# Threshold attention with a gated MLP: weights kept in their parts' storage, low words scaled on VectorE, a stacked 64-token unit, and a new planned order

## The chip, the core and the metric

The kernel runs on one core of one Trainium2 chip. The metric is the device time of one execution in microseconds (us); the time of a kernel is the median over several executions. A core has TensorE (PE in the profile; PEld are its weight loads), VectorE (DVE), ScalarE (ACT), GpSimd (POOL), and SyncE (SP), which here only issues DMA transfers.

## What is computed

The reference, cut to what matters (8 batches, 8 heads, 576 tokens, head width 64, so x is 8 x 576 x 512):

```python
scores = 0.125 * q @ k.T                                   # per head
thresh = max(scores, axis=-1) - tau
scores = where(scores >= thresh, scores, -1e9)
attn = softmax(scores);  x = attn @ v                      # heads side by side
h = gelu_tanh(x @ w_in);  u, v = h[:, :512], h[:, 512:]    # w_in: 512 x 1024
v = (v - mean(v)) / sqrt(var(v) + 1e-6) * g_ln
v = w_sg @ v + b_sg                                        # over the 576 tokens
out = x + (u * v) @ w_out                                  # w_out: 512 x 512
```

w_in and w_out arrive as 64-bit floats, and the kernel gets them as pairs of 32-bit words.

## The kernel before, in words

**Attention.** Step `attention(n)` handles two heads at once (n runs from 0 to 31, four of them make a batch). Each n has nine tiles of 128 queries by 576 keys. For a tile PE computes the scores, DVE takes the row maximum (`nm`), ACT the exponentials (`p`), POOL the threshold (written beside `nm`), and DVE multiplies by the comparison and sums (`SCALAR_TENSOR_TENSOR p`). PE then transposes `p` with an identity, ACT copies the transposed blocks out of PSUM (`pt`, `tt`), and PE multiplies by the values (`rv`) in two parts of 256 and 320 queries. The values' product has 64 output rows per head; the two heads stand in the two halves of the PE array. DVE multiplies the result by the inverse sums (`x32`), and x is split into a high part `xh` (ACT) and a rest `xl` (POOL) in the fast 32-bit format of PE.

Queries and keys are split in the same way (`qhi`, `khi` on ACT, the rest on POOL) and laid out by DMA into `qst`, `ks` and `klz`. The first n is computed without the split, straight from the loaded `rq` and `rk`.

**MLP.** `moe(b)` follows when the four attention steps of its batch are through. Units `v0` to `v3` multiply 128 tokens by the second half of w_in, `v4` the last 64 tokens; then come gelu, the normalisation and the split into `z` (`zt` for the 64 tokens). Units `u` multiply by the first half of w_in, `y` mix the tokens with `w_sg`, `o` multiply by w_out and add x. Every product of two split matrices is three matmuls: high by high, rest by high, high by rest. A unit of w_in has four blocks of 128 input columns and so 12 matmuls; `v4` has 12 too, with 64 output rows.

**Weights.** `from_double` makes the high part and the rest of one 128 x 512 block from its two words per number, 12 blocks in all: ACT takes the magnitude of the upper word (L551) and scales the low word (L552); DVE assembles the 32-bit number in four instructions (L557, L559, L561, L563); POOL multiplies the scaled low word by the number's power of two (L569) and adds it (L570); ACT copies the high part (L571) and POOL subtracts it (L572). The raw words of all 18 weight loads wait in four buffers that the `z` tiles use later.

**Order.** All steps are recorded with a nominal time. A planner (`Planner`) plays the program through with costs of its own and picks, for each engine, the next step among those that are ready, by nominal time plus an offset for the kind of step (table `OFF`, table `START` for the MLP's units). The engines execute their instructions in the order that comes out. DMA transfers are all issued by SP, in order.

Of the kernel before, what the change touches and what calls it, by code (L numbers as in the profile page):

```python
# [12 lines left out]
F32 = mybir.dt.float32  # L13
F32R = mybir.dt.float32r
# [6 lines left out]
P = 128  # L21
# [32 lines left out]
}  # L54
LAST_SCALE, SIGMA, SPREAD = 0.55, 1.155, 0.7
LOOK = dict(tensor=117.6, vector=64.6, scalar=38.8, gpsimd=48.8, sync=843.3)
# [23 lines left out]
WINDOW, WINDOW_BUSY, CLOCK, STREAM = 10240 / 3, 3200 * P, 2.4, 2.185  # L80

# [83 lines left out]
class Planner:  # L165
# [51 lines left out]
    def _record(self, engine, op, out, args, accum_out, kw):  # L217
# [26 lines left out]
        for t, entry in done:  # L244
# [5 lines left out]
                         P if engine == "tensor" else first.shape[0], engine == "vector" and ports > 1))  # L250
# [26 lines left out]
    def order(self):  # L277
# [14 lines left out]
        turn = dict(vector=0.0, gpsimd=0.0)  # L292
# [28 lines left out]
        def run(i):  # L321
# [8 lines left out]
            for k in self.steps[i]:  # L330
# [75 lines left out]
def tile_threshold_attention_gated_mlp(  # L406
# [89 lines left out]
    wih = [cpool.tile([P, DF], F32R, name=f"wih{c}") for c in range(NC)]  # L496
    wil = [cpool.tile([P, DF], F32R, name=f"wil{c}") for c in range(NC)]
    woh = [cpool.tile([P, DM], F32R, name=f"woh{c}") for c in range(NF)]
    wol = [cpool.tile([P, DM], F32R, name=f"wol{c}") for c in range(NF)]
# [31 lines left out]
    def raw_weights(k, w):  # L531
        return cpool.tile([P, 2 * FH], F32, tag=f"z{k % NM}", name=f"w{k}")[:, 0:w]

    spare = ([(mtmp, "mt0", FH), (mtmp, "mt1", FH), (mtmp, "gt0", FH)],
             [(mpool, "gh0", S), (mpool, "gl0", S), (mtmp, "gt1", FH)],
             [(mpool, "gh1", S), (mpool, "gl1", S), (xpool, "xl6", S)])

    def from_double(src, hi, lo, j, put, time, k):

        t = {}  # L540

        def load():
            t["raw"] = raw_weights(k, 2 * FH).bitcast(U32)
# [4 lines left out]
        def magnitude():  # L548
            t["full"], t["rest"], t["pow"] = (
                pool.tile([P, w], F32, tag=tag, name=f"w{k}{tag}")[:, 0:FH] for pool, tag, w in spare[j])  # L550
            nc.scalar.activation(t["full"], t["up"].bitcast(F32), AF.Abs, scale=UPPER_MORE)  # L551
            nc.scalar.activation(t["rest"], t["low"], AF.Copy, scale=2.0 ** -52)  # L552
# [16 lines left out]
        put("w_mul", time, lambda: nc.gpsimd.tensor_tensor(t["rest"], t["rest"], t["pow"], ALU.mult))  # L569
        put("w_add", time, lambda: nc.gpsimd.tensor_tensor(t["full"], t["full"], t["rest"], ALU.add))  # L570
        put("w_hi", time, lambda: nc.scalar.activation(hi, t["full"], AF.Copy))  # L571
# [683 lines left out]
```

## Time and profile before

| what | value |
|---|---|
| median of 3 runs | 1037.2 us (1036.03 to 1037.33) |
| the profiled execution | 1032.46 us, of which the span of the program's instructions is 1030.4 us |
| clock granted to TensorE, mean of the span | 0.99 |

The profiled execution is 4.7 us faster than the median of the timed runs. The profile's engine rows count a matmul as busy until its modelled end, so that consecutive matmuls overlap in the rows; the distance from start to start is what one of them costs when PE is full. "Idle before" stands for the time that an engine waited ahead of an instruction, and the arrow names what ended the wait.

### The profile page before, as it was taken

Reading aid. Unit: us, or ns where it says so; the run is one execution under the profiler, and the core shown is the slowest. Engines: PE = TensorE matmul, PEld = TensorE weight load, DVE = VectorE, ACT = ScalarE, POOL = GpSimd, SP = SyncE. Lnnn points to the kernel's source line nnn. Section 1 sums busy time; section 2 is a strip of 40 time slices with the busy share of each in tenths; the row PEclk is TensorE's granted clock in tenths of the full one; section 3 lists DMA queues with packets and bytes.
Section 4 is the critical chain, followed back from the end, with each engine's and each line's share of the span. In section 5 each row is a group of like instructions: output and inputs, shape, how many; then the busy total and the mean of one; then the engine's idle time right before and its main releaser. Section 6 shows DMA issues by size and latency. Waiting matters only on the chain.

```text
span 1030.4 us, 20086 instructions
## 1 busy us (share of the span) xinstructions
PE 973.8 (95%) x6972; PEld 836.2 (81%) x6972; DVE 654.6 (64%) x1399; ACT 695.5 (67%) x1489; POOL 617.1 (60%) x1089
## 2 busy tenths in 40 slices
PE   3768799999999999999999999999999999999997
PEld 2556578898788987889778897889878897789887
DVE  5777787755777637765576656776377655774350
ACT  4768778764877658766687648776587766865452
POOL 5878667555663666555675556645665556634566
PEclk9889999999999999999999999999999999999999
DMA  8464433444135423344144431344323441310001
GB/s 263 138 185 125 116 86 103 103 108 107 43 83 128 119 72 81 88 128 109 31 103 110 108 97 45 89 116 121 84 74 90 124 118 31 91 34 24 18 6 46
DMA packets 50758, 96.42 MB, mean 94 GB/s; under 512 B 8033, under 2 KB 16225, under 8 KB 50658
## 3 DMA queue, kind: packets, MB, share of 16 engines
q1 hardware_dynamic: 50658, 95.15, 35.0%
q8 instruction: 55, 0.90, 0.4%
q14 instruction: 45, 0.37, 0.1%
HBM read 38.44 MB, written 9.44 MB: 46 GB/s over the span
## 4 chain that ended last, share of the span: by engine, by line
PE 75%; DVE 6%; ACT 6%; POOL 6%; DMA 3%; issue 3%; SPq 1%; POOLq 0%; DVEq 0%; ACTq 0%
PE all_banks L992 37%; PE all_banks L908 13%; PE all_banks L758 13%; PE all_banks L522 12%; DVE p L800 2%; ACT pt L878 2%; POOL vv L1071 2%; ACT p L793 1%; DVE nm L767 1%; DMA qst<-qhi 1%; DMA ks<-khi 1%; POOL ot L1172 1%; DMA g_bc<-in_g_ln 1%; DVE x L920 1%; ACT vv L1068 1%
## 5 line engine op out<-in xcount | busy, mean ns | idle before, releaser
L800 DVE SCALAR_TENSOR_TENSOR p<-all_banks,nm,p 128x576 f32<-128x576 f32 x256 | 207.0, 814 | 87.7 <-ACT p L793 36.1
L767 DVE TENSOR_REDUCE nm<-all_banks 128x1 f32<-128x576 f32 x288 | 212.8, 750 | 47.7 <-PE all_banks L758 38.8
L793 ACT ACTIVATE p<-all_banks,nm 128x576 f32<-128x576 f32 x256 | 188.5, 746 | 28.4 <-DVE nm L767 27.8
L758 PE MATMUL all_banks<-ks,qst 128*128 128x288 f32 x620 | 190.3, 325 | 13.4 <-DVE p L800 5.4
L522 PE MATMUL all_banks<-ident_r,p 128*128 128x128 f32 x1152 | 173.5, 282 | 21.9 <-DVE p L800 20.5
L878 ACT ACTIVATE pt<-all_banks 128x512 f32<-128x512 f32 (+1 forms) x320 | 168.4, 557 | 29.4 <-PE all_banks L522 28.2
L758 PE MATMUL all_banks<-klz,qst 128*128 128x288 f32 x620 | 173.5, 297 | 0.0
L522 PEld LDWEIGHTS all_banks<-ident_r,p 128*128 128x128 f32 x1152 | 139.9, 145 | 38.6 <-DVE p L800 20.7
L758 PEld LDWEIGHTS all_banks<-ks,qst 128*128 128x128 f32 x620 | 118.3, 191 | 38.4 <-ACT pt L878 11.3
L908 PE MATMUL all_banks<-pt,rv 128*64 128x320 f32 (+1 forms) x1024 | 138.3, 412 | 1.1 <-ACT pt L878 1.1
L758 PEld LDWEIGHTS all_banks<-klz,qst 128*128 128x128 f32 x620 | 118.7, 191 | 0.4
L773 POOL TENSOR_TENSOR nm<-columns,nm 128x1 f32<-128x1 f32 x288 | 55.7, 197 | 100.0 <-DVE nm L767 89.8
L992 PE MATMUL all_banks<-wsh,z 128*128 128x288 f32 (+2 forms) x512 | 112.8, 296 | 0.3 <-POOL z L1084 0.3
L908 PEld LDWEIGHTS all_banks<-pt,rv 128*64 128x64 f32 x1024 | 67.8, 136 | 50.3 <-issue 8.7
L992 PEld LDWEIGHTS all_banks<-wsh,z 128*128 128x128 f32 x512 | 85.4, 188 | 0.7 <-POOL z L1084 0.5
L992 PE MATMUL all_banks<-xh,wih 128*128 128x288 f32 (+2 forms) x256 | 78.4, 306 | 3.8 <-ACT pt L878 3.8
L1144 POOL TENSOR_TENSOR gl<-uu,gh 128x288 fp32r<-128x288 f32 (+2 forms) x64 | 51.5, 807 | 49.7 <-ACT gh L1140 46.4
L978 DVE SCALAR_TENSOR_TENSOR gt<-gt,all_banks 128x512 f32<-128x512 f32 (+1 forms) x40 | 27.2, 681 | 78.4 <-ACT gt L971 78.4
L992 PE MATMUL all_banks<-xl,wih 128*128 128x288 f32 (+2 forms) x256 | 76.4, 299 | 0.0
L992 PE MATMUL all_banks<-gh,woh 128*128 128x288 f32 (+2 forms) x256 | 76.2, 298 | 0.0
L992 PE MATMUL all_banks<-xh,wil 128*128 128x288 f32 (+2 forms) x256 | 75.9, 297 | 0.0
L992 PE MATMUL all_banks<-gl,woh 128*128 128x288 f32 (+2 forms) x256 | 75.4, 295 | 0.0
(222 smaller groups left out, 2223.8 us busy)
## 6 DMA issues: line engine op xcount, KB each, us to landing
rk<-in_kT SPq DMA_DIRECT2D x32, 320.0 KB, 2.9
rv<-in_vP SPq DMA_DIRECT2D x32, 320.0 KB, 2.9
ks<-khi SPq DMA_DIRECT2D x62, 160.0 KB, 2.8
rq<-in_qT SPq DMA_DIRECT2D x32, 288.0 KB, 3.3
qst<-qhi SPq DMA_DIRECT2D x62, 144.0 KB, 2.4
qst<-rq SPq DMA_DIRECT2D x62, 144.0 KB, 2.4
ks<-khi SPq DMA_DIRECT2D x62, 144.0 KB, 2.9
out_T<-ot SPq DMA_DIRECT2D x56, 144.0 KB, 1.8
```

The lines of the kernel that those rows point to most:

```text
L522: nc.tensor.transpose(out, x, ident_r.bitcast(F32))
L758: nc.tensor.matmul(sc[:, a, 0:HALF], w, x, start=(j == 0), stop=(j == len(terms) - 1))
L767: nc.vector.tensor_reduce(nmax, st["s", h, i][:, :, 0:HALF], AX.XY, ALU.max, negate=True)
L773: nc.gpsimd.tensor_tensor(thr, toff, st["nm", h, i], ALU.subtract)
L793: nc.scalar.activation(target(h, i), st["s", h, i][:, :, 0:HALF], AF.Exp, bias=st["nm", h, i])
L800: nc.vector.scalar_tensor_tensor(dst, st["s", h, i][:, :, 0:HALF], st["thr", h, i], dst, ALU.is_ge, ALU.mult, accum_out=st["l", p][:, c:c ...
L878: nc.scalar.activation(dst, src, AF.Copy)
L908: nc.tensor.matmul(acc[h * D:(h + 1) * D, 0:w], st["v"][:, o:o + D], unit(h, p)[:, kt, 0:w] if kt < NM else tail_unit(p)[:, 0:w], start=(k ...
L978: put("stt1", end, lambda: nc.vector.scalar_tensor_tensor(t["tmp"], t["tmp"], GELU_C, t["acc"], ALU.add, ALU.mult))
L992: nc.tensor.matmul(st["acc"], *term(j), start=(j == 0), stop=(j == n - 1))
L1071: nc.gpsimd.tensor_tensor(st["v", i], st["v", i], g_bc[0:rows], ALU.mult)
L1144: nc.gpsimd.tensor_tensor(st["gl", p, d], st["u", p, d], st["gh", p, d], ALU.subtract)
```

## The change

1. The raw words of a block are loaded into the storage that its high part and rest will have (`raw_wi01` becomes `wi01`), so that the twelve loads need no shared buffers. The scratch of the conversion moves to other tiles (`wz`, `wt`).
2. The scaling of the low word on ACT and the multiply on POOL become one `scalar_tensor_tensor` on DVE (L589 of the new file), which reads the low word and the power of two.
3. xh and xl of a head pair become one tile `x` of 640 columns; the rests of the last 64 tokens are written a second time (`xt`, POOL, L956), beside their high parts. `v4` then multiplies 128 stacked rows (64 high, 64 rests) by the high weights, and 64 rows by the rests of the weights: 8 matmuls in place of 12. ACT copies the lower 64 rows of the result (`mlow`, L1001) and DVE adds them to the upper ones (`madd`, L1004) ahead of the gelu.
4. The planner adds 92 ns when PE goes to the half-array matmuls and 220 ns when it comes back; `OFF`, `START` and `LOOK` hold new numbers.
5. A few scratch tiles have other homes (the query tails, the last outputs).

```diff
-LOOK = dict(tensor=117.6, vector=64.6, scalar=38.8, gpsimd=48.8, sync=843.3)
+LOOK = dict(tensor=20.8, vector=91.4, scalar=115.7, gpsimd=100.2, sync=4015.6)
+DRAIN = (92.0, 220.0)
...
+                    if ops[k][6] != self.tiled:
+                        start += DRAIN[not ops[k][6]]
+                        self.tiled = ops[k][6]
...
-            t["raw"] = raw_weights(k, 2 * FH).bitcast(U32)
+            t["raw"] = cpool.tile([P, 2 * FH], F32, tag=home, name=f"raw_{home}").bitcast(U32)
...
-            nc.scalar.activation(t["rest"], t["low"], AF.Copy, scale=2.0 ** -52)
...
-        put("w_mul", time, lambda: nc.gpsimd.tensor_tensor(t["rest"], t["rest"], t["pow"], ALU.mult))
-        put("w_add", time, lambda: nc.gpsimd.tensor_tensor(t["full"], t["full"], t["rest"], ALU.add))
-        put("w_hi", time, lambda: nc.scalar.activation(hi, t["full"], AF.Copy))
-        put("w_lo", time, lambda: nc.gpsimd.tensor_tensor(lo, t["full"], hi, ALU.subtract))
+        put("w_mul", time, lambda: nc.vector.scalar_tensor_tensor(
+            t["pow"], t["low"], 2.0 ** -52, t["pow"], ALU.mult, ALU.mult))
+        put("w_add", time, lambda: nc.gpsimd.tensor_tensor(t["full"], t["full"], t["pow"], ALU.add))
+
+        def hi_part():
+            parts_of[home] = cpool.tile([P, 2 * FH], F32R, tag=home, name=home)
+            nc.scalar.activation(parts_of[home][:, 0:FH], t["full"], AF.Copy)
...
+                        x = x_of[b, hp] = xpool.tile([P, S + KW], F32R, tag=f"x{n % 7}", name=f"x{n}")
+                        xh_of[b, hp], xl_of[b, hp] = x[:, 0:S], x[:, KW:S + KW]
...
+                    nc.gpsimd.tensor_tensor(x_of[b, hp][:, S:KW], st["x", p][:, w - TAIL:w], xh_of[b, hp][:, MAIN:S],
+                                            ALU.subtract)
...
+        def lower_half():
+            t["h"] = tile_of()
+            nc.scalar.activation(t["h"], acc_of()[TAIL:P], AF.Copy)
+
+        def add_halves():
+            nc.vector.tensor_tensor(t["h"], acc_of()[0:TAIL], t["h"], ALU.add)
...
+            def tail_term(j):
+                c, k = divmod(j, 2)
+                if k == c // (NC - 1):
+                    return x_of[b, c][:, MAIN:KW], w_in_of(0, c, slice(FH, DF))
+                return xh_of[b, c][:, ts_], w_in_of(1, c, slice(FH, DF)), TAIL
...
+                acc = products(put, time, spread, f"v{b}_{i}", (P, FH), tail_term, 2 * NC)
```

What moves, first on DVE at the start of the program, where n = 0 is under way (`nm0_0_1` is the row maximum of head 0, tile 1; `w0`, `w1`, `w2` before and `wt1`, `wt2`, `wt3` now are weight blocks in conversion). Before:

```order
L800 SCALAR_TENSOR_TENSOR p0_0_195,l0_0_196<-all_banks_91,nm0_1_0_193,p0_0_195 128x576
L561 SCALAR_TENSOR_TENSOR w0mt0_198<-w0_164,w0mt0_198 128x512
L557 TENSOR_SCALAR w1gh0_214<-w1gh0_214 128x512
L563 TENSOR_SCALAR w0gt0_200<-w0mt0_198 128x512
L559 TENSOR_SCALAR w1gh0_214<-w1gh0_214 128x512
L557 TENSOR_SCALAR w2gh1_221<-w2gh1_221 128x512
L561 SCALAR_TENSOR_TENSOR w1gh0_214<-w1_166,w1gh0_214 128x512
L559 TENSOR_SCALAR w2gh1_221<-w2gh1_221 128x512
L563 TENSOR_SCALAR w1gt1_216<-w1gh0_214 128x512
L561 SCALAR_TENSOR_TENSOR w2gh1_221<-w2_168,w2gh1_221 128x512
L767 TENSOR_REDUCE nm0_0_1_265<-all_banks_91 128x1
```

Now, the same place:

```order
L827 SCALAR_TENSOR_TENSOR p0_0_177,l0_0_178<-all_banks_91,nm0_1_0_175,p0_0_177 128x576
L794 TENSOR_REDUCE nm0_0_1_194<-all_banks_91 128x1
L577 TENSOR_SCALAR wt1h_191<-wt1h_191 128x512
L794 TENSOR_REDUCE nm0_1_1_211<-all_banks_91 128x1
L579 TENSOR_SCALAR wt1h_191<-wt1h_191 128x512
L827 SCALAR_TENSOR_TENSOR p0_1_205,l0_0_178<-all_banks_91,nm0_0_1_194,p0_1_205 128x576
L581 SCALAR_TENSOR_TENSOR wt1h_191<-raw_wi00_153,wt1h_191 128x512
L827 SCALAR_TENSOR_TENSOR p0_1_205,l0_0_178<-all_banks_91,nm0_1_1_211,p0_1_205 128x576
L583 TENSOR_SCALAR wt1l_192<-wt1h_191 128x512
L577 TENSOR_SCALAR wt2_231<-wt2_231 128x512
L577 TENSOR_SCALAR wt3h_244<-wt3h_244 128x512
```

Nine weight instructions stood ahead of the second tile's first maximum; now none does, and the weights come between and behind. Up to the first instruction of the first MLP batch's gelu DVE executes 48 weight instructions before (all of them) and 55 now: 11 blocks with five each, the twelfth block later.

Second on SP, at the start (`rv` are values, `w0` to `w3` and `raw_wi00`, `raw_wi10` are weight loads of 512 KB each, `qst` the first laid-out queries). Before:

```order
L576 DMA g_bc_103<-in_g_ln 128x512
L546 DMA w0_164<-in_w_in 128x1024
L546 DMA w1_166<-in_w_in 128x1024
L546 DMA w2_168<-in_w_in 128x1024
L546 DMA w3_171<-in_w_in 128x1024
L658 DMA rv0_177<-in_vP 128x640
L658 DMA rv1_183<-in_vP 128x640
L697 DMA qst01_131<-qhi1_186 64x576
L697 DMA qst11_133<-qhi1_186 64x576
```

Now:

```order
L603 DMA g_bc_103<-in_g_ln 128x512
L685 DMA rv0_148<-in_vP 128x640
L685 DMA rv1_150<-in_vP 128x640
L564 DMA raw_wi00_153<-in_w_in 128x1024
L564 DMA raw_wi10_156<-in_w_in 128x1024
L724 DMA qst01_115<-qhi1_162 64x576
L724 DMA qst11_117<-qhi1_162 64x576
```

Two weight loads stand ahead of the laid-out queries where there were four.

Third on PE, the 64-token unit of the second batch. Before:

```order
L992 MATMUL all_banks_91<-wih0_104,xh4_1500 64x512
L992 MATMUL all_banks_91<-wil0_108,xh4_1500 64x512
L992 MATMUL all_banks_91<-wih0_104,xl4_1511 64x512
L992 MATMUL all_banks_91<-wih1_105,xh5_1792 64x512
L992 MATMUL all_banks_91<-wil1_109,xh5_1792 64x512
L992 MATMUL all_banks_91<-wih1_105,xl5_1816 64x512
L992 MATMUL all_banks_91<-wih2_106,xh6_2098 64x512
L992 MATMUL all_banks_91<-wil2_110,xh6_2098 64x512
L992 MATMUL all_banks_91<-wih2_106,xl6_2143 64x512
L992 MATMUL all_banks_91<-wih3_107,xh7_2866 64x512
L992 MATMUL all_banks_91<-wil3_111,xh7_2866 64x512
L992 MATMUL all_banks_91<-wih3_107,xl7_2868 64x512
```

Now (`wi01` holds the high part and the rest of one block):

```order
L1035 MATMUL all_banks_91<-wi01_950,x4_1378 128x512
L1035 MATMUL all_banks_91<-wi01_950,x4_1378 64x512
L1035 MATMUL all_banks_91<-wi11_1076,x5_1711 128x512
L1035 MATMUL all_banks_91<-wi11_1076,x5_1711 64x512
L1035 MATMUL all_banks_91<-wi21_1221,x6_2213 128x512
L1035 MATMUL all_banks_91<-wi21_1221,x6_2213 64x512
L1035 MATMUL all_banks_91<-wi31_1267,x7_2827 64x512
L1035 MATMUL all_banks_91<-wi31_1267,x7_2827 128x512
```

Four matmuls are gone, and full and half widths alternate.

More of the change, by code (lines that the diff above doesn't have):

```diff
@@ L249, in _record @@
         self.ops.append((self.current, engine, time_of(engine, op, first, reads), needs,
-                         P if engine == "tensor" else first.shape[0], engine == "vector" and ports > 1))
+                         P if engine == "tensor" else first.shape[0], engine == "vector" and ports > 1,
+                         engine == "tensor" and op != "transpose" and args[0].dtype == F32
+                         and min(first.shape[0], args[0].shape[0]) < P))
     def rehearse(self, plan):
@@ L495, in tile_threshold_attention_gated_mlp, with w_in_of, w_out_of @@
     g_bc = cpool.tile([P, FH], F32, name="g_bc")
[L496 to L499, printed above, removed]
+    parts_of = {}
+    def w_in_of(k, c, cs):
+        half = cs.start // FH
+        return parts_of[f"wi{c}{half}"][:, k * FH + cs.start - half * FH:k * FH + cs.stop - half * FH]
+    def w_out_of(k, c, ms):
+        return parts_of[f"wo{c}"][:, k * DM + ms.start:k * DM + ms.stop]
     wsh = [cpool.tile([P, S], F32R, name=f"wsh{c}") for c in range(NM)]
@@ L529, in threshold_offset, with spare, spares, from_double @@
         at("tau", 0.0, lambda: nc.vector.tensor_tensor(toff, toff, tau_sb, ALU.subtract))
[L531 to L540, printed above, removed]
+    used = [0]
+    def spare():
+        used[0] += 1
+        return used[0]
+    def spares(k, w):
+        if k % 3 == 2:
+            both = xpool.tile([P, S + KW], F32, tag="x6", name=f"wt{k}")
+            return both[:, 0:w], both[:, S:S + w]
+        return [mpool.tile([P, S], F32, tag=f"g{x}{k % 3}", name=f"wt{k}{x}")[:, 0:w] for x in "hl"]
+    def from_double(src, home, early, put, time, k):
+        t, sp = {}, None if early else spare()
         def load():
-            t["raw"] = raw_weights(k, 2 * FH).bitcast(U32)
+            t["raw"] = cpool.tile([P, 2 * FH], F32, tag=home, name=f"raw_{home}").bitcast(U32)
             words = t["raw"].rearrange("p (c w) -> p c w", w=2)
@@ L548, in magnitude @@
         def magnitude():
-            t["full"], t["rest"], t["pow"] = (
-                pool.tile([P, w], F32, tag=tag, name=f"w{k}{tag}")[:, 0:FH] for pool, tag, w in spare[j])
+            if early:
+                both = cpool.tile([P, 2 * FH], F32, tag=f"z{k % NM}", name=f"wz{k}")
+                t["full"], t["pow"] = both[:, 0:FH], both[:, FH:2 * FH]
+            else:
+                t["full"], t["pow"] = spares(sp, FH)
             nc.scalar.activation(t["full"], t["up"].bitcast(F32), AF.Abs, scale=UPPER_MORE)
-            nc.scalar.activation(t["rest"], t["low"], AF.Copy, scale=2.0 ** -52)
         def word(step):
@@ L580, in weights @@
                 cs = slice(o, o + FH)
-                jobs.append(partial(from_double, w_in[c * P:(c + 1) * P, cs], wih[c][:, cs], wil[c][:, cs], len(jobs) % 3))
+                jobs.append(partial(from_double, w_in[c * P:(c + 1) * P, cs], f"wi{c}{o // FH}", o == FH))
         for c in range(NM):
@@ L602, in tail_weights @@
     def tail_weights(put, time, k):
-        t = {}
+        t, sp = {}, spare()
         def load():
-            t["raw"] = raw_weights(k, S)
+            t["raw"] = spares(sp, S)[0]
             for d0 in (0, TAIL):
@@ L973, in gate @@
         def gate():
-            t["h"] = tile_of()
+            if not halves:
+                t["h"] = tile_of()
             nc.vector.scalar_tensor_tensor(t["h"], t["tmp"], 1.0, t["acc"], ALU.add, ALU.mult)
+        if halves:
+            put("mlow", end, lower_half)
+            put("madd", end, add_halves)
         put("msq", end, square)
@@ L991, in f @@
                 for j in range(lo, hi):
-                    nc.tensor.matmul(st["acc"], *term(j), start=(j == 0), stop=(j == n - 1))
+                    w, x, *rows = term(j)
+                    nc.tensor.matmul(st["acc"][0:rows[0]] if rows else st["acc"], w, x, start=(j == 0), stop=(j == n - 1))
             return f
@@ L1023, in w_part @@
         def w_part(cs):
-            return lambda k, c: (wih, wil)[k][c][:, cs]
+            return lambda k, c: w_in_of(k, c, cs)
         def v_unit(put, time, i):
@@ L1043, in new @@
                 return st["v", i]
-            gelu2(put, end, acc, new, f"{b}_{i}")
+            gelu2(put, end, acc, new, f"{b}_{i}", i == NM)
             def stats():
@@ L1164, in evacuate @@
                 if last and p:
-                    tag = ("x32", "y32", "ir")[m % 3]
-                    st["o", p, m] = xtmp.tile([P, S - 2 * P], F32, tag=tag, name=f"ot{b}_{p}_{m}")
+                    st["o", p, m] = xpool.tile([P, S + KW], F32, tag=f"x{4 + m % 3}", name=f"ot{b}_{p}_{m}")[:, 0:spans[p][1]]
                 else:
```

65 lines of the change are left out of this document (36 added, 29 removed), and 20 rows, old and new, of the table START.

## The prediction

> **What bounds the kernel now.** I read the busy time by stage first. The columns are the stretch, its length, then busy time and instructions of PE, PE's weight loads, DVE, ACT and POOL, the granted clock, the DMA share and GB/s:
>
> ```profile
> 0.00:20.00 20.00, 9.37 (x33) 6.13 (x33) 10.35 (x24) 8.65 (x14) 9.84 (x25) 1.00 0.87 261
> 20.00:60.00 40.00, 21.41 (x124) 15.90 (x125) 29.63 (x54) 27.05 (x53) 34.84 (x42) 0.87 0.59 168
> 60.00:134.00 74.00, 59.47 (x407) 46.86 (x408) 57.48 (x121) 56.47 (x118) 53.17 (x83) 0.93 0.47 126
> 134.00:200.00 66.00, 64.95 (x458) 52.09 (x457) 51.69 (x114) 54.41 (x118) 42.24 (x81) 1.00 0.44 109
> 200.00:980.00 780.00, 775.32 (x5667) 675.02 (x5667) 491.19 (x1060) 528.91 (x1148) 444.79 (x819) 1.00 0.33 85
> 980.00:1031.00 51.00, 43.30 (x290) 40.24 (x288) 14.29 (x30) 19.98 (x41) 32.24 (x42) 0.99 0.08 27
> ```
>
> From 134 us on PE is full: 5.7 us idle in the 846 us up to 980. There a matmul less is time saved, and DVE (63%), ACT and POOL have room. In the first 134 us PE is idle for 43.8 us (20.00 + 40 + 74 less 90.2), partly at a lower clock, and DVE, ACT and POOL are each at 69 to 73%: no engine is full, so waits between engines decide. So I read the waits of the start next, PE's first (total, times, longest), up to 140 us:
>
> ```profile
> PE all_banks L522 <- DVE p L800: 19.6, 8, 7.1
> PE all_banks L758 <- DVE p L800: 5.4, 3, 4.9
> ```
>
> PE waits above all for DVE's selected tiles. When PE gets other work, its first MLP matmul, stands in its timeline (start, length), and behind it PE is full:
>
> ```profile
> 133.81 0.48 PE L992 MATMUL all_banks<-wih,xh 128*128 128x512 f32 x1
> ```
>
> Next what DVE waits for between 9 and 134 us, and its busy time there (third number):
>
> ```profile
> DVE p L800 <- POOL nm L773: 10.0, 7, 2.9
> 9.00:134.00 125.00, 88.08 (x557) 67.28 (x554) 96.76 (x191) 90.32 (x183) 92.34 (x130) 0.92 0.55 155
> ```
>
> DVE is idle for 28.2 us there, and 10.0 of them end with POOL's threshold.
>
> **The 64-token unit.** Its 12 matmuls in the steady stage, by start and length:
>
> ```profile
> 404.25 0.29 PE L758 MATMUL all_banks<-klz,qst 128*128 128x288 f32 x1
> 404.38 0.40 PE L992 MATMUL all_banks<-wih,xh 128*64 128x512 f32 x1
> 404.62 0.39 PE L992 MATMUL all_banks<-wil,xh 128*64 128x512 f32 x1
> ...
> 406.91 0.39 PE L992 MATMUL all_banks<-wih,xl 128*64 128x512 f32 x1
> 407.14 0.33 PE L887 MATMUL all_banks<-both,pm 128*128 128x64 f32 x2
> ```
>
> From 404.38 to 407.14 are 2.76 us, or 0.23 per matmul. Full-width matmuls stand on both sides with no gap beyond a matmul's own time, so I take 0.23 for both widths. Four fewer in each of 8 batches: 32 x 0.23 = **-7.4 us**, all on PE, which is full there. In place come one ACT copy and one DVE add per batch and 32 small subtractions on POOL; nearest rows:
>
> ```profile
> L971 ACT ACTIVATE gt<-all_banks 64x512 f32<-64x512 f32 x8 | 4.7, 589 | 6.4 <-PE all_banks L992 6.4
> L978 DVE SCALAR_TENSOR_TENSOR gt<-gt,all_banks 64x512 f32<-64x512 f32 x8 | 5.4, 676 | 0.0
> L806 POOL TENSOR_SCALAR pm<-pm 64x64 f32<-64x64 f32 x32 | 7.9, 247 | 18.4 <-DVE pm L800 16.4
> L928 POOL TENSOR_TENSOR xl<-x,xh 128x256 fp32r<-128x256 f32 x32 | 23.6, 739 | 5.8 <-ACT xh L924 5.5
> ```
>
> That is 0.59 us of ACT and 0.68 of DVE per batch, and for a subtraction between 0.25 and 0.74 us; 0.33, nearer the small one, since it has 64 columns. In the steady stage this lies in the idle time of three engines that are 57 to 68% busy: 0, as long as PE has other units to work on. The added length of the unit's chain (about 1.3 us and two hand-overs) matters only in the last batch, below.
>
> At this place a rule speaks against the change: in the Trainium skill, "TensorEngine Tiling (Array Packing)", section Key Properties, a change of the array's tiling mode drains the engine. Half-width matmuls of the other kind, the values' product, do show such a gap:
>
> ```profile
> 538.87 0.29 PE L758 MATMUL all_banks<-klz,qst 128*128 128x288 f32 x1
> 539.09 2.37 PE L908 MATMUL all_banks<-pt,rv 128*64 128x320 f32 x16
> 541.29 0.71 PE L908 MATMUL all_banks<-tt,rv 128*64 128x320 f32 x4
> 541.93 0.40 PE L758 MATMUL all_banks<-ks,qst 128*128 128x288 f32 x1
> 542.17 0.30 PE L758 MATMUL all_banks<-klz,qst 128*128 128x288 f32 x1
> ```
>
> Going in costs 0.22 where 0.13 is a 288-column matmul's own (404.25 to 404.38): 0.09. Coming out, four records at 0.1375 (16 take 539.09 to 541.29) would end at 541.84 and the next starts at 541.93, and its successor 0.24 later in place of 0.13: 0.20. Together 0.29. The new unit goes full, half, full, half, full, half, half, full: three such round trips, 0.87 us, against 0.92 saved. The rows of 404 us show no gap for this kind of half-width matmul, so I take the saving and keep the other as a rival. That the planner now counts the gaps changes no matmul; there is still one round trip per part, and it gets 0.
>
> **The weights on DVE.** Sums over all twelve blocks, of L569 (POOL's multiply), L552 (ACT's scaling), then DVE's L557, L559, L561, L563; the third number is the busy time:
>
> ```profile
> 0.00:200.00 200.00, 15.52 (x12) 0.95 0.52 143
> 0.00:200.00 200.00, 8.01 (x12) 0.95 0.52 143
> 0.00:200.00 200.00, 6.81 (x12) 0.95 0.52 143
> 0.00:200.00 200.00, 8.17 (x12) 0.95 0.52 143
> 0.00:200.00 200.00, 11.73 (x12) 0.95 0.52 143
> 0.00:200.00 200.00, 6.72 (x12) 0.95 0.52 143
> ```
>
> POOL loses 15.5 us and ACT 8.0. The new DVE multiply has two SBUF inputs of 512 numbers, like L561, which lasts 0.98 on average and between these:
>
> ```profile
> 16.94 1.75 DVE L561 SCALAR_TENSOR_TENSOR w1gh<-w,w1gh 128x512 uint32<-128x512 uint32 x1
> 19.29 0.68 DVE L561 SCALAR_TENSOR_TENSOR w2gh<-w,w2gh 128x512 uint32<-128x512 uint32 x1
> ```
>
> Ahead of the first batch's gelu stand 11 blocks of five in place of 12 of four: 11 x 0.98 less 2.79 (one block's four, 33.43 / 12) is **+8.0 us** of DVE in the start. Against it:
>
> ```profile
> 23.26 1.26 POOL L569 TENSOR_TENSOR w2gl<-w2gl,w2xl 128x512 f32<-128x512 f32 x1
> 24.48 0.33 POOL L773 TENSOR_TENSOR nm<-columns,nm 128x1 f32<-128x1 f32 x2
> 24.70 0.82 DVE L800 SCALAR_TENSOR_TENSOR p<-all_banks,nm,p 128x576 f32<-128x576 f32 x1 [1.86 <-POOL nm L773]
> ```
>
> The threshold stood behind POOL's multiply, and DVE and then PE waited. Of POOL's three weight instructions a block one goes, and it is one that stood in the way; between none and all of the 10.0 us I take half, **-5.0**. Of ACT's 8.0 us I count 1.3 (it is 72% busy and seldom waited for): **-1.3**.
>
> **The order of loads.** SP now puts two weight loads ahead of the first laid-out queries and not four, 1 MB less. In the chain, with start and length, and in ACT's waits:
>
> ```profile
> 9.80 9.64 DMA qst<-qhi
> ACT khi L664 <- DMA qst<-qhi: 2.7, 1, 2.7
> ```
>
> ACT's split of k, and with it POOL behind it, waited 2.7 us for these layouts. 1 MB at the 261 GB/s of the first 20 us is 4 us, so that wait goes: **-2.7**. The loads passed come later: eight of them, 4 MB, now stand on SP ahead of the second half of n = 1's keys (`ks1_1`), which before were issued here:
>
> ```profile
> 34.99 1.43 SPq L675 DMA_DIRECT2D ks<-khi  x2
> ```
>
> If the eight were issued right ahead of it, it would land 16 us later (4 MB at 261 GB/s); since they wait for nothing but SP and the issue at 34.99 waits for PE, and the DMA share is 0.59 from 20 to 60 us, I take 0 and keep half, 8 us, for a rival. That nine weight instructions no longer stand ahead of the second tile on DVE brings PE's longest stall (7.1 us) forward, but the same instructions come later: 0 by itself.
>
> **The end.** The last batch's units come in another order, and the rest of the conversion of `v2` stands behind the new add of `v4` on DVE. Before, PE waited there, with nothing to spare, from 940 us:
>
> ```profile
> PE all_banks L992 <- POOL z L1084: 0.3, 1, 0.3
> ```
>
> A chain longer by 1.3 us, less up to 0.9 for last outputs that come one by one to POOL and not two at once: -0.9 to +2, I take **+0.5**.
>
> **Sum.** -7.4 + 8.0 - 5.0 - 1.3 - 2.7 + 0.5 = -7.9 us. Against the profiled execution (span 1030.4 and 2.1 around it, 1032.5) that is 1024.6; the median lies 4.7 higher, so 1037.2 - 7.9 = **1029 us**. Bounds: without the start's terms 1030.3. If DVE's addition falls into its 28.2 us of idle time and all 10.0 go, the start gives -14.0: 1016. If no wait goes and each multiply lasts 1.75, it gives 11 x 1.75 - 2.8 = +16.5: 1047.
>
> **Rivals.** (a) DVE becomes the bound of the start and the kernel gets slower. For it: DVE is the busiest engine between 9 and 134 us already, and L561 shows that such an instruction takes up to 1.75 beside POOL's. Between +8.0 and +16.5 stands +12: 1030.3 + 12 = 1042. It decides from a loss of 9.0 in the start on. Against it: 28.2 us idle, and the ones waited for (POOL) get lighter. The Trainium skill, "SBUF — State Buffer", section Who interferes with whom, says that a DVE instruction with two SBUF inputs and a POOL instruction that reads SBUF exclude each other, the second blocking fully; by that rule the multiply would move DVE's waits on POOL into DVE's own instructions, and the sum would be this rival's. The two L561 rows agree with it (1.75 while POOL ran, 0.68 while it didn't).
> (b) The unit's alternating widths cost 0.87 us each: -7.4 turns into -0.4, 1036. Against it: the rows at 404 us.
> (c) The lighter POOL lets the start run as DVE could: -14.0, 1016.
> (d) The eight loads delay `ks1_1`, and PE waits 8 us for it in the start: 1037, no difference. Against it: the DMA share of 0.59.
> (e) The new order puts waits into the steady stage, 7 batches x 1 us: 1036 to 1037, no difference. Against it: 5.7 us idle in 846; for it: every row of the order is new.
>
> **How the numbers follow.** Forecast (1020 to 1035) 0.51, (c) 0.15, (a) 0.18, (b) 0.06, (d) 0.05, (e) 0.05. Less than 0.2% (2.1 us) can hardly be told from no change here. Faster: 0.51 + 0.15 and a third of (b): 0.68; slower: (a) and a little of (d): 0.19; same: the rest, 0.13. From 1016 to 1041 leaves out half of (a) and half of (c). The likeliest case alone spans 1020 to 1035.
>
> **What would show it.** PE's first MLP matmul near 133 us or earlier; no gap between 128- and 64-row matmuls and 1.84 us for the unit; DVE's waits on the threshold near 5 us; the new multiply near 0.98 us; idle of PE after the start as before, under 1%. The prediction is wrong if the multiplies last 1.5 us or more, if the first MLP matmul comes after 143 us, or if the unit takes 2.7 us.

## The result, and the profile after

The changed kernel takes **1008.3 us** (median of 4 runs, 1007.4 to 1008.4) where the kernel before takes 1036.7 (1036.0 to 1037.3): a ratio of 0.9724, 95% interval 0.9707 to 0.9741. Forecast were 1029 and 1016 to 1041. The gain is 28.4 us and not 8.

By stage first, as before (stretch, its length, busy time and instructions of PE, PE's weight loads, DVE, ACT and POOL, granted clock, DMA share, GB/s):

```profile
0.00:20.00 20.00, 10.64 (x40) 7.69 (x41) 10.22 (x26) 9.09 (x15) 9.46 (x27) 1.00 0.76 233
20.00:60.00 40.00, 27.41 (x157) 21.48 (x157) 36.43 (x69) 26.42 (x53) 25.67 (x36) 0.79 0.78 232
60.00:134.00 74.00, 66.16 (x465) 51.18 (x463) 67.04 (x134) 59.30 (x127) 56.77 (x89) 0.98 0.48 123
134.00:200.00 66.00, 64.39 (x466) 52.68 (x465) 53.18 (x112) 52.54 (x115) 49.10 (x86) 1.00 0.35 88
200.00:957.00 757.00, 754.19 (x5520) 660.37 (x5519) 485.50 (x1045) 524.91 (x1135) 448.00 (x829) 1.00 0.34 88
957.00:1006.50 49.50, 43.24 (x301) 41.15 (x300) 17.91 (x37) 22.00 (x45) 33.16 (x44) 0.99 0.07 25
9.00:134.00 125.00, 101.85 (x650) 78.40 (x649) 112.92 (x220) 92.84 (x191) 85.02 (x131) 0.92 0.61 170
```

The span went from 1030.4 to 1006.5, by 23.9. PE's busy time fell by 7.8 (973.8 to 966.0), its idle time by 16.1. Of that 14.0 lie in the first 134 us (43.8 idle before; now 134 less 10.64, 27.41 and 66.16, or 29.8). In the same stretch DVE's idle time between 9 and 134 us fell from 28.2 to 12.1, although it does 16 us more work: DVE is now nearly full there. The other 4.5 of the 28.4 show in no row of the two profiles: the profiled execution of before was its fastest (1032.5; 59 runs of it in the comparisons below, on five chips, lie between 1033.1 and 1039.9), while that of the changed kernel lies at its median.

What PE waits for in the start (total, times, longest), its first MLP matmul, DVE's waits on the threshold, and the new multiplies (12, their busy time third):

```profile
PE all_banks L535 <- DVE p L827: 10.3, 9, 2.7
PE all_banks L785 <- DMA ks<-khi: 5.1, 1, 5.1
124.67 1.17 PE L1035 MATMUL all_banks<-wi,x 128*128 128x512 f32 x4
DVE p L827 <- POOL nm L800: 1.5, 1, 1.5
0.00:200.00 200.00, 8.38 (x12) 0.95 0.53 144
```

The waits for DVE's selected tiles fell from 25.0 to 10.3, the longest from 7.1 to 2.7. The first MLP matmul comes at 124.67 and not at 133.81. The threshold's 10.0 are 1.5, and a multiply lasts 0.70 on average. New is a wait of 5.1 us for the keys of n = 1.

The steady stage, by the start of the 64-token unit in the second and the seventh batch; first before, then now (x2 there, since the window ends inside the unit), and the unit of the third batch with the row behind it:

```profile
284.46 0.40 PE L992 MATMUL all_banks<-wih,xh 128*64 128x512 f32 x1
885.79 0.40 PE L992 MATMUL all_banks<-wih,xh 128*64 128x512 f32 x1
```
```profile
268.70 0.62 PE L1035 MATMUL all_banks<-wi,x 128*128 128x512 f32 x2
863.16 0.61 PE L1035 MATMUL all_banks<-wi,x 128*128 128x512 f32 x2
387.43 1.99 PE L1035 MATMUL all_banks<-wi,x 128*128 128x512 f32 x8
389.26 0.29 PE L785 MATMUL all_banks<-ks,qst 128*128 128x288 f32 x1
```

A batch took (885.79 - 284.46) / 5 = 120.27 us and takes (863.16 - 268.70) / 5 = 118.89. The unit takes 1.83 us (387.43 to 389.26) for eight matmuls of alternating widths, 0.23 each: no drain.

### The profile page after: what moved, and what is told of

Read it like the earlier page. It is cut to its first block, busy times and chain, and to the rows that moved or that the text cites. A ratio compares the mean times of both kernels' runs of the same rounds, so it can differ in the third digit from the quotient of the medians.

```text
span 1006.5 us, 20067 instructions
## 1 busy us (share of the span) xinstructions
PE 966.0 (96%) x6940; PEld 834.5 (83%) x6940; DVE 670.3 (67%) x1419; ACT 694.3 (69%) x1485; POOL 622.1 (62%) x1109
## 4 chain that ended last, share of the span: by engine, by line
PE 70%; POOL 9%; ACT 7%; DMA 5%; DVE 4%; issue 3%; SPq 1%; POOLq 0%; ACTq 0%; DVEq 0%
PE all_banks L1035 35%; PE all_banks L785 13%; PE all_banks L535 11%; PE all_banks L935 11%; POOL z L1136 2%; POOL vv L1123 2%; ACT pt L905 1%; ACT vv L1120 1%; DVE p L827 1%; POOL bn L1112 1%; DMA wt<-in_w_sgT 1%; ACT z L1129 1%; POOL x L953 1%; DMA qst<-qhi 1%; ACT p L820 1%
## 5 line engine op out<-in xcount | busy, mean ns | idle before, releaser
L794 DVE TENSOR_REDUCE nm<-all_banks 128x1 f32<-128x576 f32 x288 | 215.1, 752 | 74.6 <-PE all_banks L785 63.0
L820 ACT ACTIVATE p<-all_banks,nm 128x576 f32<-128x576 f32 x256 | 188.2, 744 | 31.3 <-DVE nm L794 30.1
L535 PE MATMUL all_banks<-ident_r,p 128*128 128x128 f32 x1152 | 174.8, 281 | 11.4 <-DVE p L827 8.9
L1035 PE MATMUL all_banks<-x,wi 128*128 128x288 f32 (+2 forms) x768 | 120.4, 299 | 0.0
L800 POOL TENSOR_TENSOR nm<-columns,nm 128x1 f32<-128x1 f32 x288 | 60.5, 217 | 91.3 <-DVE nm L794 87.0
L1035 PE MATMUL all_banks<-wsh,z 128*128 128x288 f32 (+2 forms) x512 | 115.2, 300 | 0.3 <-ACT z L1129 0.3
L1223 POOL TENSOR_TENSOR ot<-ot,x 128x288 f32<-128x288 f32 (+2 forms) x128 | 102.6, 806 | 14.4 <-ACT ot L1220 9.2
L1035 PE MATMUL all_banks<-gh,wo 128*128 128x288 f32 (+2 forms) x512 | 111.5, 300 | 0.0
L1035 PE MATMUL all_banks<-wi,x 128*128 128x512 f32 x448 | 109.3, 393 | 0.4 <-DVE uu L1014 0.4
L1035 PEld LDWEIGHTS all_banks<-x,wi 128*128 128x128 f32 x768 | 106.2, 188 | 0.8 <-issue 0.5
L1035 PEld LDWEIGHTS all_banks<-wi,x 128*128 128x128 f32 x448 | 80.2, 184 | 18.1 <-DVE uu L1014 0.8
```

What stands on the lines that cost most here:

```text
L535: nc.tensor.transpose(out, x, ident_r.bitcast(F32))
L794: nc.vector.tensor_reduce(nmax, st["s", h, i][:, :, 0:HALF], AX.XY, ALU.max, negate=True)
L800: nc.gpsimd.tensor_tensor(thr, toff, st["nm", h, i], ALU.subtract)
L820: nc.scalar.activation(target(h, i), st["s", h, i][:, :, 0:HALF], AF.Exp, bias=st["nm", h, i])
L1035: nc.tensor.matmul(st["acc"][0:rows[0]] if rows else st["acc"], w, x, start=(j == 0), stop=(j == n - 1))
L1223: return lambda: nc.gpsimd.tensor_tensor(o(), o(), x[b, m][:, ts_], ALU.add)
```

## The experiments

The question: where do 20 us more than forecast come from? Three theories stood at first. **L**: POOL's multiplies stood in the way (the prediction's rival c). **O**: the order puts the weight work behind the attention's. **S**: raw words in their own storage hold up no load. Any edit makes the planner choose anew and moves thousands of rows. So most kernels here **keep an order**: the plan is made from the unedited steps, and the edit acts only when the steps are issued in it; besides the rows named, every engine's rows stay as they were. The diffs are cut to what matters, some of their lines put in words. Each is given by its ratio to runs of before on the same chip; a difference of ratios times 1036.7 is in us, and the two intervals together make that uncertain by 2 to 3 us.

### One part at a time in the old order

The stacked unit (b_unit), own storage (b_store), and with it the multiply on DVE (b_mul):

```diff
-                    nc.tensor.matmul(st["acc"], *term(j), ...)           # 12 of 64 columns
+                    nc.tensor.matmul(st["acc"][0:rows[0]] ..., w, x, ...) # 8, as in the change; copy and add in the step "msq"
```
```diff
-            t["raw"] = raw_weights(k, 2 * FH).bitcast(U32)
+            t["raw"] = cpool.tile([P, 2 * FH], F32, tag=home, name=f"raw_{home}").bitcast(U32)
```
```diff
-            nc.scalar.activation(t["rest"], t["low"], AF.Copy, scale=2.0 ** -52)
-            nc.gpsimd.tensor_tensor(t["rest"], t["rest"], t["pow"], ALU.mult)
+            nc.vector.scalar_tensor_tensor(t["rest"], t["low"], 2.0 ** -52, t["pow"], ALU.mult, ALU.mult)
```

> The order of the kernel before, instruction by instruction, with the stacked 64-token unit alone (8 matmuls for 12; the copy, the add and the small subtraction stand where the unit's first gelu step and the second rest stood). The prediction's term: -7.4 us (1029). If the alternating widths drained PE by 0.87 us per batch: -0.4 (1036). Since the order is kept, what a free planner would do with the gap is not in it; a loss of 1 to 2 us at the end would show as -5 to -6.

> The order of the kernel before, with the raw words of each block loaded into the block's own storage in place of the four shared buffers; nothing else. Theory S (the start got shorter because loads no longer wait on SP for the words of older blocks): -5 us or more. Theories O (the order did it) and L (the lighter POOL did it): no difference, -1 to +1, since the instructions that use the words keep their places.

> As the run with own storage, and besides the multiply of the low word on VectorE and not on POOL, without ACT's scaling, at the place in the order where POOL's multiply stood. Theory L (POOL's 12 multiplies stood in the way): -8 to -14 against the run with own storage alone. The prediction's terms (+8.0 on DVE, -5.0 and -1.3 for the lighter POOL and ACT): +1.7. Theory O: -2 to +3, since the weight work still stands ahead of the same tiles.

Measured: the unit **1043.9** (1.0069, 1.0051 to 1.0087), 0.7% slower; own storage **1035.4** (0.9989, 0.9975 to 1.0003); with the multiply **1037.8** (1.0009, 0.9997 to 1.0022). Theory S alone falls. The multiply costs 0.0020 or 2 us, hardly more than the uncertainty; the prediction's terms for it, +8.0 - 5.0 - 1.3, give +1.7. What happened is seen in DVE's waits, in its stretch from 9 to 134 us and in PE's waits, first own storage, then the multiply:

```profile
DVE p L812 <- POOL nm L785: 11.1, 7, 2.6
9.00:134.00 125.00, 89.11 (x528) 66.40 (x525) 90.79 (x180) 87.53 (x177) 88.66 (x124) 0.81 0.54 153
PE all_banks L533 <- DVE p L812: 17.9, 8, 7.6
```
```profile
DVE p L815 <- POOL nm L788: 2.1, 3, 1.1
9.00:134.00 125.00, 91.35 (x531) 68.28 (x528) 98.83 (x192) 81.72 (x165) 77.35 (x114) 0.85 0.54 154
PE all_banks L533 <- DVE p L815: 18.5, 9, 5.5
```

POOL lost 11 us of work and the threshold's waits went from 11.1 to 2.1, but DVE got 8 us more, and PE waits for its tiles as long as before, 18.5 us after 17.9. Theory L falls for the old order.

The unit's matmuls did last 1.84, yet PE waited more. DVE's add, its waits and those behind it in b_unit:

```profile
L980 DVE TENSOR_TENSOR vv<-all_banks,vv x8: 681/683/684, 189.4 to 1001.1; 64x512 f32<-64x512 f32 x8
  ACT vv L979: 9.9, 8
  ACT gt L983: 6.1, 8
```

DVE stood 9.9 us for ACT's copy and ACT 6.1 for the add. So a further kernel spread the steps, each at the next one's place:

```diff
-        put("msq", end, square)                     # copy, add and square together
+        put("msq", end, lambda: lower_half() if late() else square())
+        put("stt1", end, lambda: add_halves() if late() else scaled())   # and so on
```

> The order of the kernel before with the stacked unit, as in the run that came out 7 us slower; there DVE's add waited 9.9 us in all right behind ACT's copy, and ACT's next instruction 6.1 us for the add. Here the unit's steps are spread: the copy stands where the first gelu step stood, the add at the second's place, and so on, so that each finds its input done. The prediction's term, once nothing is blocked: -5 to -7.4 us against 1036, 1029 to 1031. If the unit costs that much by itself: 1042 or more.

Measured: **1046.8** (1.0094, 1.0077 to 1.0111). The add waits for nothing there, so the blocking by the copy is not the cause. PE waits 2 to 8 us behind the unit for an attention tile, in b_unit for ACT's copy of one (1.23 us), in b_unit2 here:

```profile
298.75 0.66 PE L524 MATMUL all_banks<-ident_r,p 128*128 128x128 f32 x4 [1.58 <-DVE p L803]
```

Before has no such wait at this place. Adding up the rows of PE's waits from 134 us on gives 6.4 us before, 21.6 in b_unit and 21.9 in b_unit2: 15 us more, where 7.4 us of matmuls went. That the four matmuls were the cover of DVE's and ACT's work there is my reading; shown is only that in the old order 0.92 us less on PE came back as more wait.

### The weights behind the attention, in the old order

The work of the first three blocks goes behind the first attention's fourth select; b_defer with the shared buffers, bs_defer with own storage:

```diff
+    move(words + multiplies, adds, roundings, rests of blocks 0 to 2 that stood ahead of it, behind select 3)
```

> The order of the kernel before, but all work of the first three weight blocks on DVE, POOL and ACT's rounding that stood ahead of the fourth select of the first attention is put behind that select; nothing else changes. The prediction costed this reordering at 0 by itself: -1 to +1. Theory O: the first attention's tiles 1 come some 6 us earlier on DVE, and -4 to -7 of it lasts. Theory L: about 0 (POOL has as much to do).

> The order of the kernel before, own storage for the raw words, and the work of the first three weight blocks put behind the fourth select of the first attention: the two edits that gave -1.3 and +7.6 us alone. Theory O+S (the order gains, but only once waiting words hold up no load on SP): 6 us or more below the run with own storage alone, so 1030 or less. If the late weights themselves cost (theory L or a later wait for weights): about 1040 or more.

Measured: **1044.3** (1.0081, 1.0064 to 1.0099) and **1046.3** (1.0086, 1.0066 to 1.0106), 8 to 9 us slower. With the shared buffers a load stood on SP for the words that had not been read:

```profile
SPq L547 <- DVE w0mt L562: 11.9, 1, 11.9
```

Own storage frees SP and gains nothing. "Weights later" as such is not what the new order gains by: theory O in this form falls.

### Parts undone in the new order

The old unit (a_12b; a_12 is a first form), the multiply back on POOL and the scaling on ACT (a_pool), and both (a_12pool):

```diff
-                    w, x, *rows = term(j)                         # 8, two widths
+                    nc.tensor.matmul(st["acc"], *whole(j), ...)   # 12 of 64 columns
```
```diff
-            nc.vector.scalar_tensor_tensor(t["pow"], t["low"], 2.0 ** -52, t["pow"], ALU.mult, ALU.mult)
+            nc.scalar.activation(t["low"].bitcast(F32), t["low"], AF.Copy, scale=2.0 ** -52)
+            nc.gpsimd.tensor_tensor(t["pow"], t["low"].bitcast(F32), t["pow"], ALU.mult)
```

> The order of the changed kernel, instruction by instruction, with the old 64-token unit: 12 half-width matmuls in place of 8, without the copy, the add and the small subtractions. The prediction's term: 32 x 0.23 us more, 1008.3 + 7.4 = 1015.7. If the widths drained PE by 0.87 us per batch: 1008.7. If the unit's longer chain cost waits in the steady stage, as the unit alone did in the old order (+7.2), taking it out gains them back: 1008 or less.

> The order of the changed kernel, instruction by instruction, with 12 half-width matmuls in the 64-token unit in place of 8; every other instruction stays (ACT's copy writes zeros, which DVE adds), so that only PE's work changes. The prediction's term: 1008.3 + 32 x 0.23 = 1015.7. Alternating widths that drain PE by 0.87 us per batch: 1008.7.

> The order of the changed kernel, with the multiply back on POOL at the same place and the scaling of the low word back on ACT (in place). Theory L (the lighter POOL let the start run): +5 to +10 us over 1008.3. The prediction's terms taken back: -8.0 + 5.0 + 1.3 = -1.7. Theory O+S: -3 to +3, since DVE is the fullest engine of the start now (112.9 of 125 us) and POOL has room.

> The same, and the multiply back on POOL with ACT's scaling: of the change only the order and the own storage are left. If the parts add (unit 7.4, multiply 6.3 in this order): 1022, and the order with its storage alone is worth 14 to 15 us against 1036.7. If the two parts' costs overlap: 1016 to 1019.

Measured: a_12 1022.2; it computes other numbers, probably because the gelu reads PSUM longer than the plan had kept the bank, and it is left out. a_12b **1013.3** (0.9790, 0.9765 to 0.9815): the unit is worth 0.0066, 6.8 us, in this order. a_pool **1014.7** (0.9787, 0.9769 to 0.9805): the multiply on DVE is worth 6.5 us here, as theory L had it, where it cost 2 in the old order. Whether POOL or ACT made the 6.5 is not separated, since both get their work back. Both undone, **1018.4** (0.9828, 0.9806 to 0.9851): 10.8 of the gain go, less than 6.8 + 6.5, and **17.8 stay with the order, its own storage and its scratch tiles**, which no run takes apart. The stretch from 9 to 134 us in a_12pool, to be set beside the kernel with own storage in the old order, which has the same weight and attention work there:

```profile
9.00:134.00 125.00, 96.80 (x631) 72.68 (x630) 106.16 (x206) 96.66 (x197) 92.80 (x140) 0.92 0.59 170
```

DVE is idle for 18.8 us in place of 34.2, and PE for 28.2 in place of 35.9; PE gets through 631 matmuls there in place of 528. The profile of own storage is its slowest run, at a clock of 0.81; the row of before, at 0.92, has 28.2 and 36.9 us of idle time and 557 matmuls.

### What in the order

Weights first on SP and DVE as before, with ACT's magnitudes for them (a_hoist), the multiply right behind a block's last word (a_mulnow), and with it the add, the rounding and the rest (a_nowait):

```diff
+    move(four weight loads, ahead of the values);  move(nine words, ahead of the second tile's maximum)
```
```diff
+    for each block: move(w_mul [, w_add, w_hi, w_lo], behind its last w_word)
```

> The order of the changed kernel, but four weight loads ahead of the values on SP and the first nine weight instructions of DVE ahead of the second tile's maximum, as in the kernel before (with the roundings of ACT that they need). The prediction: +2.7 for the loads and 0 for the DVE order, 1011. Theory O+S: +5 to +9 us, 1013 to 1017. Theory L: 1008 to 1011.

> The same for DVE's multiply alone; POOL's and ACT's work keeps its place. If DVE's order among weights and attention does not matter as long as DVE is full (as the run with nine weight instructions put first showed): -1 to +1. If the waiting multiply is the gain: +3 us or more.

> The order of the changed kernel, but each weight block's multiply, add, rounding and rest stand right behind its last word instruction on their engines (before, POOL's multiply came at most 7 us behind that word; now up to 42 us pass). If the order gains because weight work waits until the attention's work is through POOL, ACT and DVE: +5 us or more, with DVE's waits for POOL's threshold back at 4 us or more. If the waiting itself is worth nothing: -2 to +2.

Measured: a_hoist **1008.3** (0.9723), no difference, where theories O and S together wanted +5 to +9; a_mulnow **1016.5** (0.9806, 0.9788 to 0.9824), 8.5 us slower; a_nowait **1051.0** (1.0145, 1.0123 to 1.0168), **some 43 us** slower, and slower than before. ACT's split of n = 1's keys, first in the changed kernel, then in a_hoist, shows that the loads did move it:

```profile
16.41 0.74 ACT L691 ACTIVATE khi<-rk 128x640 fp32r<-128x640 f32 x1 [0.50 <-DMA qst<-rq]
```
```profile
19.05 0.76 ACT L692 ACTIVATE khi<-rk 128x640 fp32r<-128x640 f32 x1
```

So 2.6 us earlier were worth nothing. In a_nowait, POOL's, ACT's, DVE's and PE's waits between 9 and 134 us:

```profile
POOL wz L592 <- DVE wz L590: 7.7, 4, 2.8
POOL wt L592 <- DVE wt L590: 5.2, 2, 2.9
ACT wi L596 <- POOL wz L592: 9.2, 4, 4.1
DVE p L828 <- POOL nm L801: 10.5, 4, 3.5
PE all_banks L536 <- DVE p L828: 14.2, 9, 5.2
PE all_banks L536 <- POOL ir L851: 13.8, 2, 8.4
```

The chain of a block goes DVE, POOL, ACT, POOL. Put close together, each link reaches the head of its engine before its input is there, and the attention's inverses, thresholds and copies stand behind it. Adding up the rows of the waits whose waiting instruction is a weight one (POOL, ACT and DVE, 9 to 134 us): before 10.7 + 11.4 + 3.8 = 25.9 us, in the changed kernel 4.5 + 8.2 + 2.0 = 14.7, in a_nowait 24.7 + 31.3 + 6.0 = 62.0. In the changed kernel 3 to 42 us pass between a block's last word and its multiply (before at most 2.5, not the 7 of the expectation). The multiply reads the raw low word, which own storage keeps until then. What the waiting buys against a_nowait is that a link finds its input done.

That is not the whole account. In a_mulnow the same sum is 1.5 + 5.5 + 1.9 = 8.9 us, less than in the changed kernel, and it is 8.5 us slower; in a_ks11b below it is 20.9, and the time is the same. So these waits do not set the time by themselves. In a_mulnow the multiplies stand ahead of the attention on DVE and last longer, and PE waits more for DVE's tiles:

```profile
0.00:200.00 200.00, 11.43 (x12) 0.95 0.52 144
PE all_banks L536 <- DVE p L828: 13.7, 10, 4.1
```

A multiply lasts 0.95 there on average, not 0.70. Shown is thus that in the new order the place of a block's links is worth 8.5 to 43 us; that the 17.8 us against the old order come from the same is not shown.

Is it the numbers of the tables? The changed code with the old numbers (a_beforetab), the old code with the new ones (b_aftertab), and the changed code and new numbers with the four shared buffers and old scratch tiles (a_shared), each planned anew:

```diff
-OFF, START, LOOK, DRAIN of one kernel
+those of the other (mlow, madd: as msq; xt: as xl)
```
```diff
-            t["raw"] = cpool.tile([P, 2 * FH], F32, tag=home, ...)
+            t["raw"] = raw_weights(k, 2 * FH).bitcast(U32)
```

> The changed kernel's code (own storage, multiply on DVE, stacked unit), ordered anew with the numbers of the kernel before (OFF, START, LOOK, no drains; the three new kinds get the numbers of their neighbours). If the code makes the gain and any planning finds it: 1005 to 1012. If the numbers of the tables, that is the order, make it: 1025 to 1040, 1029 being the prediction's sum for the code.

> The code of the kernel before, ordered anew with the numbers of the changed kernel (OFF, START, LOOK). If the new numbers are better for any code: 1015 to 1025 (the order is worth 14 to 18 us and nothing else changes). If numbers and code belong together, as the changed code with the old numbers showed (1056): 1045 or more.

> The changed kernel with the raw words back in the four shared buffers and with the old scratch tiles, ordered anew with the same tables (DVE's first rows still put the attention ahead of the weights). Theory O+S (waiting words must not hold up loads on SP): 1018 or more, with SP waiting for DVE words and PE for the attention's inputs behind them. If storage does not matter: 1005 to 1012.

Measured: **1056.1** (1.0187, 1.0161 to 1.0213), **1055.2** (1.0182, 1.0162 to 1.0202) and **1059.7** (1.0228, 1.0205 to 1.0252). Neither code nor numbers gain alone: 1036.7 and 1008.3 for matching pairs, 1055 to 1056 for crossed ones. The three lose at different places. From 9 to 134 us, in the order of the runs above:

```profile
9.00:134.00 125.00, 78.74 (x459) 55.83 (x458) 102.22 (x180) 73.57 (x147) 75.68 (x108) 0.80 0.49 143
9.00:134.00 125.00, 96.11 (x581) 73.03 (x577) 95.12 (x189) 89.98 (x186) 82.94 (x128) 0.85 0.57 160
9.00:134.00 125.00, 96.88 (x587) 70.66 (x585) 97.20 (x199) 85.82 (x175) 75.44 (x124) 0.88 0.56 159
```

a_beforetab loses in the start (459 matmuls, before 557). The two with the new numbers and the shared buffers get through more there than before, and lose behind it, as their stretches from 134 to 200 us show, where before is idle for 1.1 us and they for 8.1 and 10.5:

```profile
134.00:200.00 66.00, 57.86 (x433) 44.56 (x433) 53.86 (x118) 53.02 (x116) 37.57 (x72) 1.00 0.51 131
134.00:200.00 66.00, 55.50 (x383) 42.12 (x384) 55.73 (x111) 48.73 (x104) 37.91 (x73) 0.97 0.46 117
```

In a_shared SP does not wait long for words (1.8 us at most in one row), so what I expected there is not its cause; PE's longest wait from 134 us on is one of 7.9 us, for the 64-token unit's `zt`:

```profile
PE all_banks L1038 <- POOL zt L1141: 7.9, 1, 7.9
```

All three are other orders, so they do not show what own storage is worth in the new order; whether another order would do for shared buffers stays open too.

### The new long wait

PE's 5.1 us for n = 1's keys come from eight weight loads ahead of them on SP. The keys go ahead of all eight (a_ks11), or of the last five (a_ks11b):

```diff
+    move([loads[i] for i in (8, 1, 2, 3, 4, 15, 16, 17)], steps("k_place1")[0], True)   # a_ks11b: (3, 4, 15, 16, 17)
```

> The order of the changed kernel, but the two DMAs of the second half of n = 1's keys are issued ahead of the eight weight loads (4 MB) that stand before them on SP. The wait of PE for them (5.1 us, the longest in the start) goes: rival (d) of the prediction says -4 to -5 us, 1003 to 1004. If DVE is what bounds the start, PE only waits elsewhere: -1 to +1.

> The order of the changed kernel, but the two DMAs of the second half of n = 1's keys go ahead of the last five of the eight weight loads (2.5 MB), not of all eight: the first three loads, which ACT's next weight instruction needs, keep their time. Putting them ahead of all eight cost 4.4 us because that ACT instruction then waited 7.0 us for its load with the attention's copies behind it. If PE's 5.1 us wait is worth something once no other queue is blocked: -2 to -5 us, 1003 to 1006. If DVE bounds the start anyway: -1 to +1. If the later loads block again: +2 or more.

Measured: **1012.8** (0.9771, 0.9753 to 0.9789), 4.9 us slower; **1009.4** (0.9734, 0.9716 to 0.9752), no difference. In a_ks11 the wait moved, ACT's row first, then PE's:

```profile
ACT wz L573 <- DMA raw_wi<-in_w_in: 7.0, 1, 7.0
PE all_banks L536 <- ACT tt L925: 7.7, 1, 7.7
```

A weight instruction at ACT's head waited for its load, and PE for the copy behind it. Without that blocking, in a_ks11b, the wait for the keys is gone and nothing is gained: PE waits 14.3 us for DVE's tiles in place of 10.3. None of the kernels tried is measurably faster than the changed one.

## Why the prediction was wrong, step by step

- **The reordering, 0: the step that failed.** For the nine instructions at DVE's second tile 0 was right (a_hoist). For the work of three blocks in the old order it was not: putting it later cost 8 us (b_defer). And the order as a whole had no term, while it is worth 17.8 us with its storage. I summed engine work in the start (what DVE gets, what POOL loses) and took the order's rows as moves of equal work. The start had three engines at 69 to 73% and 28 us of idle DVE, so waits between engines decide, as the prediction itself says; it then priced only some of them. What in the order makes the 17.8 stays open; a_nowait and a_mulnow show only that the place of the blocks' links is part of what the new order depends on.
- **The weights on DVE, +8.0 - 5.0 - 1.3.** The multiply lasts 0.70, not 0.98, so the +8.0 were 11 x 0.70 - 2.79 = 4.9; with the multiplies right behind their words (a_mulnow) 0.95 did come. The threshold gave 8.5 of its 10.0, not 5.0. In the old order the sum came out (+2 measured, +1.7 forecast) partly by luck: there the threshold's waits fell by 9.0, and PE's for DVE's tiles did not fall. In the new order the move gains 6.5. One number for an edit was wrong, for it depends on the order around it. A slip beside it: L561 lasts up to 1.89 (at 51.07 us), not 1.75.
- **The loads, -2.7.** The split of k came 3.1 us earlier (19.55 to 16.41) and that was worth 0.
- **The 64-token unit, -7.4.** 1.84 us as forecast, and 6.8 in the new order. That PE is full was not enough for it: in the old order the same unit made the kernel 7 to 10 us slower, by 15 us more of PE's waits.
- **The steady stage, 0, and the end, +0.5.** A batch got 1.38 us shorter, 0.92 by the unit. From the seventh batch's unit to the end 144.6 us became 143.3. Two units lie in that stretch, whose own saving is 1.84, so the end cost 0.6, near the +0.5.
- **The rivals.** (a) did not come: DVE is the fullest engine of the start, but idle time took the multiplies. (b) fell with the 1.83. (c) gave the nearest time (1016); that its 14.0 equals the 14.0 of PE's idle time is chance, for it was added up from DVE's waits and from ACT's work and waits. Its reason, the lighter POOL, held only in the new order, for at most 6.5 us. (d) came as a 5.1 us wait and cost nothing. (e) fell: from 134 to 957 us PE is idle for 4.4 us.
- **The base.** 4 of the 20 us: the sum was made against an execution that was faster than all other runs of before, and the offset to their median was carried over.

## What to carry to other kernels

Where no engine is full, do not price a planner's new order by the work that it moves: look, engine by engine, at the instructions that wait at the head of their queue and at what stands behind them, and expect that an order and the code for which it was found may gain only together. Here a preparation that ran beside such a start wanted its links apart, in storage of their own: putting them together cost 43 us. A removed wait, or work taken from a full engine, may come back as a wait for something else, as the keys and the old order's unit did; test it by putting one part back in an unchanged order, and count all of PE's waits, not those of one kind.

## What the runs showed of the hardware

Executions of one kernel differ in the granted clock: the mean of the span lay between 0.976 and 0.990 in the 59 runs of before. In the profile of before it was 0.87 from 20 to 60 us and 0.93 from 60 to 134; in the kernel with own storage, whose order is the same and whose profile is its slowest run, it was 0.71 and 0.87:

```profile
20.00:60.00 40.00, 23.54 (x123) 17.55 (x123) 28.85 (x52) 26.75 (x53) 34.18 (x42) 0.71 0.55 164
60.00:134.00 74.00, 59.03 (x378) 45.35 (x379) 52.15 (x112) 54.11 (x113) 50.15 (x78) 0.87 0.46 123
```

All runs of before spread over 7.4 us (1032.5 to 1039.9). The time follows the mean clock only loosely: on one chip 1036.7 came at 0.989 and 1035.1 at 0.980. The four runs of the changed kernel lie within 1.0 us, too few to set beside that. The Trainium skill, "TensorE: Matmul & The Clock Gate", section What's actually happening, has a clock that follows recent activity in a window that runs freely and does not start with the kernel; the runs agree in that one kernel gets different clocks; none shows where such a window stands.

Of two DVE instructions with two SBUF inputs and 512 columns, the multiply lasted 0.70 on average and the word's third step 1.06 (12.72 us for 12) in the same kernel. The Trainium skill, "SBUF — State Buffer", section Who interferes with whom, says that such an instruction and a POOL one that reads SBUF exclude each other. The rows agree, and they show who pays: the third step at 60.78 us starts while a subtraction of POOL runs and lasts 1.69, the multiply at 27.85 starts ahead of one and lasts 0.68.

```profile
0.00:200.00 200.00, 12.72 (x12) 0.95 0.53 144
60.51 1.41 POOL L718 TENSOR_TENSOR rq<-rq,qhi 128x576 fp32r<-128x576 f32 x1 [2.10 <-ACT qhi L691]
60.78 1.69 DVE L581 SCALAR_TENSOR_TENSOR wz<-raw_wi,wz 128x512 uint32<-128x512 uint32 x1
27.85 0.68 DVE L589 SCALAR_TENSOR_TENSOR wt<-raw_wi,wt 128x512 f32<-128x512 uint32 x1
27.94 1.20 POOL L953 TENSOR_TENSOR x<-x,x 128x256 fp32r<-128x256 f32 x1 [0.40 <-ACT x L951]
```

So the price depends on where in the order it stands.
